# Weighted sums of v by plain f32 matmuls, two heads side by side in TensorE's columns, with separate denominators, in a linear-attention and two-layer feed-forward kernel

## The chip, the cores and the metric

The kernel runs on one core of a Trainium2 chip, as one program. The metric is device microseconds from the first to the last instruction. Three runs of the kernel before took 1057.39, 1061.38 and 1066.32 us; the median is 1061.38 us.

## The reference

Attention with exponential features instead of a softmax, then a gated feed-forward layer, then a second one with a leaky ReLU. Batch 4, 8 heads, 576 positions, head width 64, 128 projected features; all in float32.

```python
def phi(x):
    proj = np.einsum('bhsd,df->bhsf', x, w_phi)
    proj = proj - np.max(np.abs(proj), axis=-1, keepdims=True)
    return np.concatenate([np.exp(proj), np.exp(-proj)], axis=-1)
q_p, k_p = (phi(q), phi(k))
kv = np.einsum('bhsf,bhsd->bhfd', k_p, v)
z = np.sum(k_p, axis=2)
num = np.einsum('bhsf,bhfd->bhsd', q_p, kv)
den = np.einsum('bhsf,bhf->bhs', q_p, z)[..., None] + 1e-06
attn = num / den                                  # -> x: 2304 tokens x 512
gate = 1.0 / (1.0 + np.exp(-(x @ w_gate)))
x = gate * (x @ w_val) @ w_out                    # d_ff 1536
h = x @ w_in2
out = np.maximum(0.01 * h, h) @ w_out2            # d_ff 2048
```

## The kernel before

The program has two parts. The first, up to about 290 us, is attention, with most of the first chunk of the gated layer filled in between (pieces `M`, `up1` L205 and `down1` L235). The second part is the rest of both feed-forward layers; nothing of it is edited.

Attention works on 16 pairs of heads, 4 for each batch entry. The two heads of a pair lie together in most tiles. For each pair: k and q are loaded and transposed on TensorE (`transposed`, L324); multiplied with w_phi, which stands as a block diagonal for the two heads (`proj`, L337), with the row maximum and its subtraction on VectorE; k's features are exponentials on ScalarE (`features`, L352). `kv_main` (L389) sums k's features times v, and times a column of ones, over the positions: for each sign `s` of the exponent and each head one block of 128 features by 65 columns, 64 of v and one that holds the sum z. q's projections are transposed back and exponentiated (`q_f`, L410), so that features lie in partitions and the 576 positions in columns.

Then `num` (L433) multiplies: stationary is the block of `kv` (128 features; 65 columns used and 63 of zeros, so that the array's 128 columns are all taken), moving are 288 positions of q's features. The product has the weighted sums of v in 64 partitions and the denominator in a 65th. It is made for each head, each half `n` of the positions, and accumulated over the two signs: 8 products for a pair. For the second head the ones stand ahead of v, so that its sums land in partitions 64 to 127.

Precision comes in two forms. In a plain form, operands are float32. In the split form each operand is a rounded part (type float32r) and a remainder; `mm3` (L51) adds three matmuls (high x low weights and so on) and `split` (L47) makes the parts, the high one by a copy on ScalarE and the remainder by a subtraction on VectorE. `PLAIN_N` (L254) names the 8 of 16 pairs whose products in `num` are plain; the other 8 are split, for which `q_f` makes the exponentials twice on ScalarE (`qh` rounded, `qa` in full) and the remainder `ql` on VectorE (L430), and `kv_main` splits the block (`kvzr`).

`norm1` to `norm3` follow: the denominators are reshaped by a small DMA from one partition to 64 (tile `d`), 1e-6 is added and the reciprocal taken on VectorE, the result goes through DRAM and comes back broadcast over partitions (`rb`), GpSimd multiplies, and `norm3` splits the result into `xh` and `xl`, the feed-forward input.

The order of the pieces is a table: `ORDERS` holds lists of piece names (`tk` transposes k, `pk0` projects, `nn0` to `nn3` are the four steps of `num`, `nm1` to `nm3` the norm steps, `M` a unit of the gated layer, `d` a step of weight decoding, `ld` the next loads), `SLOTS` says which list each of 17 slots takes. In slot i the features of pair i, the sums of pair i-1 and `norm3` of pair i-2 are issued. The framework's scheduler reorders within each engine by its own estimate, so the engines' lists differ from the table. PSUM tiles of attention: a ring of three buffers `at` (transposes, projections), and `kv0`, `kv1` with one each, which the kv sums and the products of `num` share.

Of the kernel before, what the change touches and what calls it, by code (L numbers as in the profile page):

```python
# [19 lines left out]
def linear_attention_moe(ctx, tc, q, k, v, w_phi, w_gate, w_val, w_out, w_in2, w_out2, out):  # L20
# [233 lines left out]
    PLAIN_P, PLAIN_N = {0, 2}, {0, 1, 2, 3, 4, 5, 12, 14}  # L254
# [19 lines left out]

    kvzs = {}
    for nm, dts in (("f", (F32,)), ("r", (F32R, F32R))):
        kvzs[nm] = []
        for i in range(1):
            z = [wk.tile([128, 2, 256], dt, name=f"kvz{nm}{i}{j}") for j, dt in enumerate(dts)]
            for t in z:  # L280
                if nm == "f":
                    nc.gpsimd.memset(t[:, :, 65:128], 0.0)
                else:
                    nc.gpsimd.tensor_copy(t[:, :, 65:128], kvzs["f"][i][0][:, :, 65:128])
            kvzs[nm].append(z)
# [103 lines left out]
    def kv_main(p, s):  # L389

        ps = ps_a.tile([128, 2, 65], F32, tag=f"kv{s}", name="kv")
        vf = nat["v", p.b, p.c]
        for j in range(J):
            for h in range(2):
                nc.tensor.matmul(ps[:, h], p.kf[j // 2][:, j % 2, h, s, :], vf[:, j, 64 * h:64 * h + 65], start=(h, j) == (0, 0), stop=False)  # L395
        nc.tensor.matmul(ps.rearrange("p h w -> p (h w)"), rem["k"][:, 0, p.c % 2, s, :], vf[:, J], start=False, stop=True)
        zs = kvzs["f" if KD * p.b + p.c in PLAIN_N else "r"]
        p.kvz = zs[(KD * p.b + p.c) % len(zs)]
        part = [t[:, s].rearrange("p (h w) -> p h w", h=2)[:, :, 0:65] for t in p.kvz]
        if len(part) == 1:  # L400
            nc.scalar.copy(part[0], ps)
        else:
            split(ps, *part)
# [6 lines left out]
    def q_f(p, h):  # L410
# [8 lines left out]
        for sc in (1.0, -1.0):  # L419
            if KD * p.b + p.c in PLAIN_N:  # L420
                qf = wk.tile([128, S], F32, tag="qh", name="qf", bufs=4)
                exps(qf, sc)
                p.qf.append((qf,))
                continue
# [8 lines left out]
    def num(p, h):  # L433
        uh = wk.tile([128, S], F32, tag=f"u{h}", name=f"u{h}", bufs=2)
        for n in range(2):
            if n:
                yield
            cs = slice(288 * n, 288 * n + 288)
            ps2 = ps_a.tile([128, 288], F32, tag=f"kv{n}", name="ps_n")
            for s in range(2):  # L440
                i = 2 * h + s
                w = [z[:, s, 65 * h:65 * h + 128] for z in p.kvz]
                x = [f[:, cs] for f in p.qf[i]]
                if len(w) == 1:
                    nc.tensor.matmul(ps2, w[0], x[0], start=s == 0, stop=s == 1)  # L445
                else:
                    mm3(ps2, *w, *x, s == 0, s == 1)
            nc.scalar.copy(uh[:, cs], ps2)
        p.u.append(uh)

    def norm1(p):
        p.d = wk.tile([128, 9], F32, tag="d", name="d", bufs=2)
        for h in range(2):
            nc.sync.dma_start(out=p.d[64 * h:64 * h + 64], in_=p.u[h][64 - h:65 - h, :])

    def norm2(p):
        r = wk.tile([128, 9], F32, tag="r", name="r", bufs=2)
        nc.vector.tensor_scalar_add(p.d, p.d, 1e-6)
        nc.vector.reciprocal(r, p.d)
# [16 lines left out]
    def new_pair(b, c):  # L476
        p = Pair()
        p.b, p.c = b, c
        p.kf, p.tq, p.qf, p.u = [], [], [], []
# [25 lines left out]
    def step(gen, k=1):  # L505
# [15 lines left out]
    ]  # L521
    SLOTS = [0, 1, 2, 1, 5, 4, 3, 6, 3, 4, 3, 4, 3, 6, 5, 6, 3]
# [4 lines left out]
    for i in range(NP + 1):  # L527
# [9 lines left out]
        for piece in ORDERS[SLOTS[i]].split():  # L537
# [8 lines left out]
            elif piece[:2] == "nn":  # L546
                if o:
                    if piece[2:] in ("0", "2"):
                        ln = num(o, int(piece[2]) // 2)
# [499 lines left out]
```

## Time and profile before

| what | value |
|---|---|
| median of 3 runs | 1061.38 us |
| span of the profiled execution, its only time | 1055.6 us |
| busy share PE / PEld / DVE / ACT / POOL | 97% / 82% / 74% / 49% / 16% |
| mean granted TensorE clock | 0.997 |

The profile names engines PE (TensorE matmuls), PEld (its weight loads), DVE (VectorE), ACT (ScalarE), POOL (GpSimd), SP (SyncE, which issues DMAs). Busy time of matmuls includes the time in flight, and matmuls overlap, so how often one starts says more than how long one takes. A plain f32 matmul leaves two records, each with its own weight load; a transpose and an fp32r matmul leave one.

### The profile page before, as it was taken

To read this page: it belongs to the slowest core of one execution; us is meant where nothing else is said; L and a number is where in the kernel's file an instruction comes from. 1 tells how busy PE (TensorE), PEld (TensorE's weight loads), DVE (VectorE), ACT (ScalarE), POOL (GpSimd) and SP (SyncE) were. 2 spreads that over 40 slices of the span, in tenths; PEclk is the share of its full clock that TensorE was granted. 3 is DMA by queue.
4 is the path that set the end of the run, shared out by engine and by line. 5 is a ranking of instruction groups with operands and counts; after the bars stand their busy time and mean duration, and the time that the engine had idled before them with its cause. 6 is when DMAs were issued, how large, how long until landed. Compare 5 with 4: busy or idle time off the path is not lost.

```text
span 1055.6 us, 15004 instructions
## 1 busy us (share of the span) xinstructions
PE 1024.2 (97%) x5410; PEld 870.9 (82%) x5410; DVE 779.7 (74%) x1373; ACT 519.4 (49%) x1066; POOL 170.2 (16%) x217
## 2 busy tenths in 40 slices
PE   8999999999999989999999999899999999999998
PEld 7788989889788778888888878688888888888886
DVE  4964878766489748396684959998797887979555
ACT  4766676767456535454454434477343333433221
POOL 0112121212201123324144120001010010101000
PEclk9999999999999999999999999999999999999999
DMA  6543344332287978759499494536161542515143
GB/s 146 157 98 90 88 101 108 82 104 75 74 296 226 343 141 246 114 145 262 73 239 195 82 317 182 182 139 228 52 237 71 171 149 91 178 62 179 42 165 133
DMA packets 119481, 160.06 MB, mean 152 GB/s; under 512 B 68720, under 2 KB 71408, under 8 KB 119408
## 3 DMA queue, kind: packets, MB, share of 16 engines
q1 hardware_dynamic: 95216, 94.09, 28.5%
q0 software_dynamic: 24192, 65.02, 24.6%
q8 instruction: 43, 0.70, 0.3%
q14 instruction: 30, 0.25, 0.1%
HBM read 109.64 MB, written 49.36 MB: 151 GB/s over the span
## 4 chain that ended last, share of the span: by engine, by line
PE 81%; DVE 8%; DMA 5%; ACT 3%; issue 2%; SPq 1%; POOL 1%; POOLq 0%; DVEq 0%; ACTq 0%
PE ps_u L53 11%; PE ps_u L52 11%; PE ps_u L54 11%; PE ps_p L52 11%; PE ps_p L54 11%; PE ps_p L53 11%; PE kv L395 4%; PE ps_n L445 2%; DMA raw<-in_moe_w_gate_dram 1%; DMA acc<-xd 1%; PE ps_t L328 1%; DVE w L750 1%; DVE ql L430 1%; DVE acc L739 1%; DMA w<-td 1%
## 5 line engine op out<-in xcount | busy, mean ns | idle before, releaser
L831 DVE TENSOR_TENSOR q<-ps_u,q 128x512 f32<-128x512 f32 x160 | 109.6, 686 | 65.6 <-PE ps_u L54 59.4
L53 PE MATMUL ps_u<-xl,w 128*128 128x512 f32 (+1 forms) x432 | 151.6, 351 | 0.3 <-DVE xl L686 0.3
L52 PE MATMUL ps_u<-xh,w 128*128 128x512 f32 (+1 forms) x432 | 151.4, 351 | 0.1
L54 PE MATMUL ps_u<-xh,w 128*128 128x512 f32 (+1 forms) x432 | 150.9, 350 | 0.0
L901 DVE TENSOR_TENSOR acc<-acc,ps_p 128x512 f32<-128x512 f32 x126 | 86.1, 684 | 39.6 <-PE ps_p L54 39.0
L52 PE MATMUL ps_p<-w,gh 128*128 128x512 f32 x288 | 112.2, 390 | 0.0
L53 PE MATMUL ps_p<-w,gh 128*128 128x512 f32 x288 | 112.0, 389 | 0.0
L54 PE MATMUL ps_p<-w,gl 128*128 128x512 f32 x288 | 111.7, 389 | 0.0
L791 POOL DMA_DIRECT2D w<-td x88 | 48.7, 560 | 380.6 <-PE ps_u L54 365.2
L679 POOL DMA_DIRECT2D accd<-w x80 | 70.8, 892 | 229.2 <-ACT w L678 148.3
L52 PE MATMUL ps_u<-w 128*128 128x512 f32 x256 | 100.2, 391 | 1.6 <-DVE q L831 1.6
L53 PE MATMUL ps_u<-w 128*128 128x512 f32 x256 | 99.9, 390 | 0.7 <-DMA w<-td 0.7
L54 PE MATMUL ps_u<-w 128*128 128x512 f32 x256 | 99.7, 389 | 0.0
L52 PEld LDWEIGHTS ps_u<-xh,w 128*128 128x128 f32 x432 | 81.9, 190 | 11.9 <-DVE q L831 0.5
L53 PEld LDWEIGHTS ps_u<-xl,w 128*128 128x128 f32 x432 | 82.0, 190 | 11.4 <-DVE xl L686 0.5
L54 PEld LDWEIGHTS ps_u<-xh,w 128*128 128x128 f32 x432 | 81.9, 190 | 10.9
L52 PE MATMUL ps_p<-gh,w 128*128 128x512 f32 (+1 forms) x216 | 79.3, 373 | 10.3 <-ACT gh L48 4.8
L467 POOL TENSOR_TENSOR rb<-u,rb 64x576 f32<-64x576 f32 x32 | 49.2, 1537 | 233.8 <-DMA rb<-rd 136.3
L717 ACT ACTIVATE q<-q 128x512 f32<-128x512 f32 x48 | 30.2, 632 | 111.9 <-DVE q L831 111.6
L53 PE MATMUL ps_p<-gl,w 128*128 128x512 f32 (+1 forms) x216 | 80.1, 372 | 0.4 <-DVE gl L49 0.4
L54 PE MATMUL ps_p<-gh,w 128*128 128x512 f32 (+1 forms) x216 | 79.7, 370 | 0.0
L49 DVE TENSOR_TENSOR gl<-q,gh 128x512 fp32r<-128x512 f32 (+1 forms) x102 | 61.8, 613 | 20.6 <-ACT gh L48 20.2
(151 smaller groups left out, 2306.0 us busy)
## 6 DMA issues: line engine op xcount, KB each, us to landing
w<-td POOLq DMA_DIRECT2D x88, 512.0 KB, 6.5
td<-w SPq DMA_DIRECT2D x32, 512.0 KB, 5.2
accd<-w POOLq DMA_DIRECT2D x64, 256.0 KB, 6.1
raw<-in_moe_w_out_dram SPq DMA_DIRECT2D x28, 512.0 KB, 4.8
raw<-in_moe_w_in_dram SPq DMA_DIRECT2D x16, 512.0 KB, 4.1
raw<-in_moe_w_gate_dram SPq DMA_DIRECT2D x12, 512.0 KB, 5.9
raw<-in_moe_w_val_dram SPq DMA_DIRECT2D x12, 512.0 KB, 5.1
rb<-rd SPq DMA_DIRECT2D x32, 144.0 KB, 3.2
```

The source lines that it names most:

```text
L49: nc.vector.tensor_tensor(out=lo, in0=src, in1=hi.bitcast(F32), op=ALU.subtract)
L52: nc.tensor.matmul(ps, lh, rh, start=first, stop=False, **kw)
L53: nc.tensor.matmul(ps, lh, rl, start=False, stop=False, **kw)
L54: nc.tensor.matmul(ps, ll, rh, start=False, stop=last, **kw)
L395: nc.tensor.matmul(ps[:, h], p.kf[j // 2][:, j % 2, h, s, :], vf[:, j, 64 * h:64 * h + 65], start=(h, j) == (0, 0), stop=False)
L445: nc.tensor.matmul(ps2, w[0], x[0], start=s == 0, stop=s == 1)
L467: nc.gpsimd.tensor_tensor(out=p.rb[sl], in0=p.u[h][sl], in1=p.rb[sl], op=ALU.mult)
L679: nc.gpsimd.dma_start(out=accd[b][:, e], in_=st, accum_op=ALU.add)
L717: nc.scalar.activation(out=th, in_=t, func=ACTF.Lrelu)
L791: nc.gpsimd.dma_start(out=ts[n][k][0].bitcast(F32), in_=td[l, pair, n][:, k])
L831: nc.vector.tensor_tensor(out=o, in0=x, in1=y, op=ALU.add)
L901: nc.vector.tensor_tensor(out=a, in0=a, in1=po, op=ALU.add)
```

## The change

All 16 pairs become plain in `num`: `PLAIN_N`, the zero-padded tiles `kvzs`, the second exponentials and the remainders are gone. A matmul of `num` now has 64 stationary columns, the sums alone; the first head writes partitions 0 to 63 of a PSUM tile and the second 64 to 127, so they take different columns of the array, and the list alternates between the heads. The denominators get matmuls of their own: z of one head and sign, repeated in 32 columns, gives 32 equal partitions; head and sign choose which quarter of the columns. Nothing is accumulated over the signs there: both are copied to `dd`, fetched into two tiles `d0` and `d1`, and added on VectorE. The multiplication on GpSimd is one for both heads. The four steps of `num` are now two of sums and two of denominators.

```diff
@@ kv_main @@
-        zs = kvzs["f" if KD * p.b + p.c in PLAIN_N else "r"]
-        p.kvz = zs[(KD * p.b + p.c) % len(zs)]
-        part = [t[:, s].rearrange("p (h w) -> p h w", h=2)[:, :, 0:65] for t in p.kvz]
-        if len(part) == 1:
-            nc.scalar.copy(part[0], ps)
-        else:
-            split(ps, *part)
+        if s == 0:
+            p.kvz = wk.tile([128, 2, 2, 65], F32, tag="kvz", name="kvz", bufs=2)
+        nc.scalar.copy(p.kvz[:, s], ps)
@@ q_f @@
-            a = wk.tile([128, S], F32, tag="qa", name="qa", bufs=2)
-            qh = wk.tile([128, S], F32R, tag="qh", name="qh", bufs=4)
-            ql = wk.tile([128, S], F32R, tag="ql", name="ql", bufs=4)
-            exps(qh, sc)
-            exps(a, sc)
-            nc.vector.tensor_tensor(out=ql, in0=a, in1=qh.bitcast(F32), op=ALU.subtract)
-            p.qf.append((qh, ql))
+            qf = wk.tile([128, S], F32, tag="qf", name="qf", bufs=6)
+            exps(qf, sc)
+            p.qf.append(qf)
@@ num @@
-            ps2 = ps_a.tile([128, 288], F32, tag=f"kv{n}", name="ps_n")
-            for s in range(2):
-                i = 2 * h + s
-                w = [z[:, s, 65 * h:65 * h + 128] for z in p.kvz]
-                x = [f[:, cs] for f in p.qf[i]]
-                if len(w) == 1:
-                    nc.tensor.matmul(ps2, w[0], x[0], start=s == 0, stop=s == 1)
-                else:
-                    mm3(ps2, *w, *x, s == 0, s == 1)
-            nc.scalar.copy(uh[:, cs], ps2)
+    HS = [(h, s) for s in range(2) for h in range(2)]
...
+        for n, cs in enumerate(halves):
+            ps2 = ps_a.tile([128, 288], F32, tag=f"kv{n}", name="ps_n")
+            for h, s in HS:
+                nc.tensor.matmul(ps2[64 * h:64 * h + 64], p.kvz[:, s, h, h:h + 64], p.qf[2 * h + s][:, cs], start=s == 0, stop=s == 1)
+            nc.scalar.copy(p.u[:, cs], ps2)
+            yield
+        p.dd = wk.tile([128, S], F32, tag="dd", name="dd", bufs=2)
+        for n, cs in enumerate(halves):
+            ps3 = ps_a.tile([128, 288], F32, tag="at", name="ps_d", bufs=3)
+            for h, s in HS:
+                i = 2 * h + s
+                z = p.kvz[:, s, h, 64 * (1 - h):64 * (1 - h) + 1].to_broadcast([128, 32])
+                nc.tensor.matmul(ps3[32 * i:32 * i + 32], z, p.qf[i][:, cs], start=True, stop=True)
+            nc.scalar.copy(p.dd[:, cs], ps3)
+            yield
@@ norm1, norm2 @@
-        p.d = wk.tile([128, 9], F32, tag="d", name="d", bufs=2)
-        for h in range(2):
-            nc.sync.dma_start(out=p.d[64 * h:64 * h + 64], in_=p.u[h][64 - h:65 - h, :])
+        p.d = [wk.tile([128, 9], F32, tag=f"d{s}", name=f"d{s}", bufs=2) for s in range(2)]
+        for s in range(2):
+            for h in range(2):
+                i = 32 * (2 * h + s)
+                nc.sync.dma_start(out=p.d[s][64 * h:64 * h + 64], in_=p.dd[i:i + 1, :])
...
-        nc.vector.tensor_scalar_add(p.d, p.d, 1e-6)
+        nc.vector.scalar_tensor_tensor(out=p.d[0], in0=p.d[0], scalar=1e-6, in1=p.d[1], op0=ALU.add, op1=ALU.add)
...
-        for h in range(2):
-            sl = slice(64 * h, 64 * h + 64)
-            nc.gpsimd.tensor_tensor(out=p.rb[sl], in0=p.u[h][sl], in1=p.rb[sl], op=ALU.mult)
+        nc.gpsimd.tensor_tensor(out=p.rb, in0=p.u, in1=p.rb, op=ALU.mult)
@@ tables @@
-    SLOTS = [0, 1, 2, 1, 5, 4, 3, 6, 3, 4, 3, 4, 3, 6, 5, 6, 3]
+    SLOTS = [0, 1, 1, 2, 3, 4, 5, 6, 5, 4, 3, 4, 3, 7, 3, 3, 8]
```

`ORDERS` is rewritten, with nine lists in place of seven. Slots 1 and 2 have no `d` any more, slot 3 has all of them, and what is left is issued ahead of slot 4; from slot 4 on `M` stands 69 times in place of 64.

TensorE's list around the products of pair 8 (the first of batch entry 2), before. `ps_n` is the PSUM tile of a product, `qh`, `ql` and `kvzr` its split operands, `ps_p` a projection of the next pair, `pv` a tile of the gated layer:

```order
L53 MATMUL ps_n_1988<-ql_1888,kvzr00_140 128x288
L52 MATMUL ps_p_2004<-wbh_113,xhi_1968 128x256
L53 MATMUL ps_p_2004<-wbl_114,xhi_1968 128x256
L54 MATMUL pv_2351<-xh10_82,w_399 128x512
L54 MATMUL ps_n_1988<-qh_1887,kvzr01_141 128x288
L52 MATMUL ps_n_1996<-qh_1879,kvzr00_140 128x288
L53 MATMUL ps_n_1996<-ql_1880,kvzr00_140 128x288
L54 MATMUL ps_n_1996<-qh_1879,kvzr01_141 128x288
L52 MATMUL ps_n_1996<-qh_1887,kvzr00_140 128x288
L53 MATMUL ps_n_1996<-ql_1888,kvzr00_140 128x288
```

And of the changed kernel, the same pair. `ps_d` is the tile of the denominators; the four `qf` of a tile are head 0 and 1 with the first sign, then with the second:

```order
L416 MATMUL ps_n_1973<-qf_1884,kvz_1915 64x288
L416 MATMUL ps_n_1973<-qf_1899,kvz_1915 64x288
L416 MATMUL ps_n_1973<-qf_1887,kvz_1915 64x288
L416 MATMUL ps_n_1973<-qf_1902,kvz_1915 64x288
L416 MATMUL ps_n_1979<-qf_1884,kvz_1915 64x288
L416 MATMUL ps_n_1979<-qf_1899,kvz_1915 64x288
L416 MATMUL ps_n_1979<-qf_1887,kvz_1915 64x288
L416 MATMUL ps_n_1979<-qf_1902,kvz_1915 64x288
L425 MATMUL ps_d_1986<-qf_1884,kvz_1915 32x288
L425 MATMUL ps_d_1986<-qf_1899,kvz_1915 32x288
L425 MATMUL ps_d_1986<-qf_1887,kvz_1915 32x288
L425 MATMUL ps_d_1986<-qf_1902,kvz_1915 32x288
```

In place of three matmuls for each of eight products there are eight matmuls of 64 columns and eight of 32 (four more stand a few rows further down). Here the eight are unbroken; over the whole list the 128 matmuls of 64 columns stand in 38 runs and those of 32 columns in 30, with 124 changes of width.

VectorE's list where pair 8 gets its features, before. `m` is a row maximum, `t` and `tq` the projections less that, `kvzr01` the remainder of the kv block, `xlo` a remainder of the next pair's transposed k or q:

```order
L349 TENSOR_TENSOR tq_1862<-ps_p_1853,m_1860 128x512
L49 TENSOR_TENSOR kvzr01_141<-kv_1925,kvzr00_140 128x2x65
L430 TENSOR_TENSOR ql_1880<-qa_1878,qh_1879 128x576
L430 TENSOR_TENSOR ql_1888<-qa_1886,qh_1887 128x576
L430 TENSOR_TENSOR ql_1911<-qa_1909,qh_1910 128x576
L430 TENSOR_TENSOR ql_1919<-qa_1917,qh_1918 128x576
L49 TENSOR_TENSOR kvzr01_141<-kv_1951,kvzr00_140 128x2x65
L49 TENSOR_TENSOR xlo_1969<-ps_t_1963,xhi_1968 128x512
```

And of the changed kernel:

```order
L337 TENSOR_TENSOR tq_1854<-ps_p_1845,m_1852 128x512
L439 RECIPROCAL r_1817<-d0_1796 128x9
L335 TENSOR_REDUCE m_1863<-ps_p_1856 128x4
L337 TENSOR_TENSOR t_1865<-ps_p_1856,m_1863 128x512
L49 TENSOR_TENSOR xlo_1960<-ps_t_1954,xhi_1959 128x512
```

The six subtractions between the last projection and the next pair's `xlo` are gone; the reciprocal and a projection of k stand there.

## Rows read from the trace of the kernel before

**Rows 1.** The page, part 1: busy us (share of the span) x instructions

```profile
PE 1024.2 (97%) x5410; PEld 870.9 (82%) x5410; DVE 779.7 (74%) x1373; ACT 519.4 (49%) x1066; POOL 170.2 (16%) x217
```

**Rows 2.** Busy time by stretch: us, busy us (x instructions) by engine, clock, DMA

```profile
20.00:60.00 40.00, 35.53 (x226) 29.30 (x226) 34.76 (x67) 28.26 (x72) 2.95 (x2) 1.00 0.55 137
60.00:285.00 225.00, 218.35 (x1530) 196.44 (x1530) 152.78 (x282) 145.86 (x399) 45.32 (x30) 1.00 0.35 91
285.00:1055.60 770.60, 753.54 (x3580) 630.62 (x3579) 585.13 (x1012) 338.79 (x584) 119.91 (x169) 1.00 0.59 170
```

**Rows 3.** The chain in order of time, end of attention: start us, us

```profile
290.17 0.60 ACT st L226
...
290.78 0.32 SPq L229
...
291.15 6.49 DMA raw<-in_moe_w_gate_dram
...
297.67 0.43 DVE e L102
```

**Rows 4.** Waits of PE, 20 to 285 us: total us, times, longest us

```profile
PE ps_n L53 <- DVE ql L430: 2.1, 3, 1.2
...
PE ps_n L445 <- ACT qf L416: 1.3, 2, 0.7
PE ps_p L52 <- DVE xl L49: 1.2, 1, 1.2
...
PE ps_n L54 <- DVE kvzr L49: 0.9, 1, 0.9
```

**Rows 5.** Groups: busy us, mean ns of one | idle us before, releasers

```profile
L395 PE MATMUL kv<-vf,ka 128*128 128x65 f32 x512 | 63.2, 270 | 0.0
...
L467 POOL TENSOR_TENSOR rb<-u,rb 64x576 f32<-64x576 f32 x32 | 49.2, 1537 | 233.8 <-DMA rb<-rd 136.3 <-ACT qa L417 38.9 <-DVE xlo L49 18.0
...
L445 PE MATMUL ps_n<-qf,kvzf 128*128 128x288 f32 x128 | 37.8, 412 | 1.4 <-ACT qf L416 1.3
...
L430 DVE TENSOR_TENSOR ql<-qa,qh 128x576 fp32r<-128x576 f32 x32 | 34.6, 1096 | 18.8 <-ACT qa L416 12.5 <-ACT qa L417 6.2
...
L448 ACT COPY u<-ps_n 128x288 f32<-128x288 f32 x64 | 27.0, 441 | 16.5 <-PE ps_n L54 9.6 <-PE ps_n L445 6.6
...
L416 ACT ACTIVATE qa<-ps_q 128x512 f32<-128x512 f32 x32 | 21.0, 657 | 0.5 <-DVE ql L430 0.5
...
L52 PE MATMUL ps_n<-qh,kvzr 128*128 128x288 f32 x64 | 20.0, 315 | 0.0
...
L53 PE MATMUL ps_n<-ql,kvzr 128*128 128x288 f32 x64 | 19.6, 309 | 2.1 <-DVE ql L430 2.1
...
L54 PE MATMUL ps_n<-qh,kvzr 128*128 128x288 f32 x64 | 19.2, 302 | 0.9 <-DVE kvzr L49 0.9
...
L417 ACT ACTIVATE qa<-ps_r 128x64 f32<-128x64 f32 x32 | 9.3, 290 | 0.0
...
L49 DVE TENSOR_TENSOR kvzr<-kv,kvzr 128x130 fp32r<-128x130 f32 x16 | 4.6, 290 | 5.9 <-ACT kvzr L48 5.9
```

**Rows 6.** Tile ps_n: duration ns min/median/max, first and last start us

```profile
L445 PE MATMUL ps_n<-qf,kvzf x128: 403/406/510, 22.9 to 261.0; 128*128 128x288 f32 x128
```

**Rows 7.** Timeline of PE: start us, us; a run's last is in it

```profile
42.84 1.62 PE L445 MATMUL ps_n<-qf,kvzf 128*128 128x288 f32 x6
44.30 0.60 PE L328 MATMUL ps_t<-ident,q 128*128 128x128 f32 x4
...
48.83 2.34 PE L395 MATMUL kv<-vf,ka 128*128 128x65 f32 x20
```

**Rows 8.** Timeline of PE, fp32r products of one pair, every one a row

```profile
125.32 0.29 PE L53 MATMUL ps_n<-ql,kvzr 128*128 128x288 f32 x1
...
126.91 0.29 PE L53 MATMUL ps_n<-ql,kvzr 128*128 128x288 f32 x1
```

**Rows 9.** DMA issues: KB each, median us to landing

```profile
d<-u SPq DMA_DIRECT2D x32, 2.2 KB, 2.0
```

More of the change, by code (lines that the diff above doesn't have):

```diff
@@ L250, in linear_attention_moe @@
     ps_a = att.enter_context(tc.tile_pool(name="ps_a", bufs=1, space=PS))
-    PLAIN_P, PLAIN_N = {0, 2}, {0, 1, 2, 3, 4, 5, 12, 14}
+    PLAIN_P = {0, 2}
     wbd = wk.tile([128, 2 * NF], F32, name="wbd")
@@ L273, in linear_attention_moe @@
         vfs.append(vf)
[L275 to L282, printed above, removed]
-                else:
-                    nc.gpsimd.tensor_copy(t[:, :, 65:128], kvzs["f"][i][0][:, :, 65:128])
-            kvzs[nm].append(z)
     nat = {}
@@ L430, in q_f @@
-            nc.vector.tensor_tensor(out=ql, in0=a, in1=qh.bitcast(F32), op=ALU.subtract)
-            p.qf.append((qh, ql))
[L433 to L438, printed above, removed]
-            ps2 = ps_a.tile([128, 288], F32, tag=f"kv{n}", name="ps_n")
-            for s in range(2):
-                i = 2 * h + s
-                w = [z[:, s, 65 * h:65 * h + 128] for z in p.kvz]
-                x = [f[:, cs] for f in p.qf[i]]
-                if len(w) == 1:
-                    nc.tensor.matmul(ps2, w[0], x[0], start=s == 0, stop=s == 1)
-                else:
-                    mm3(ps2, *w, *x, s == 0, s == 1)
-            nc.scalar.copy(uh[:, cs], ps2)
-        p.u.append(uh)
@@ L451, in norm1, with num @@
-    def norm1(p):
-        p.d = wk.tile([128, 9], F32, tag="d", name="d", bufs=2)
-        for h in range(2):
-            nc.sync.dma_start(out=p.d[64 * h:64 * h + 64], in_=p.u[h][64 - h:65 - h, :])
+            qf = wk.tile([128, S], F32, tag="qf", name="qf", bufs=6)
+            exps(qf, sc)
+            p.qf.append(qf)
+    HS = [(h, s) for s in range(2) for h in range(2)]
+    def num(p):
+        p.u = wk.tile([128, S], F32, tag="u", name="u", bufs=2)
+        halves = [slice(288 * n, 288 * n + 288) for n in range(2)]
+        for n, cs in enumerate(halves):
+            ps2 = ps_a.tile([128, 288], F32, tag=f"kv{n}", name="ps_n")
+            for h, s in HS:
[6 more added lines that the diff above has]
+            for h, s in HS:
+                i = 2 * h + s
+                z = p.kvz[:, s, h, 64 * (1 - h):64 * (1 - h) + 1].to_broadcast([128, 32])
+                nc.tensor.matmul(ps3[32 * i:32 * i + 32], z, p.qf[i][:, cs], start=True, stop=True)
+            nc.scalar.copy(p.dd[:, cs], ps3)
+            yield
@@ L456, in norm2 @@
+    def norm1(p):
+        p.d = [wk.tile([128, 9], F32, tag=f"d{s}", name=f"d{s}", bufs=2) for s in range(2)]
[3 more added lines that the diff above has]
+                nc.sync.dma_start(out=p.d[s][64 * h:64 * h + 64], in_=p.dd[i:i + 1, :])
     def norm2(p):
         r = wk.tile([128, 9], F32, tag="r", name="r", bufs=2)
-        nc.vector.tensor_scalar_add(p.d, p.d, 1e-6)
-        nc.vector.reciprocal(r, p.d)
+        nc.vector.scalar_tensor_tensor(out=p.d[0], in0=p.d[0], scalar=1e-6, in1=p.d[1], op0=ALU.add, op1=ALU.add)
+        nc.vector.reciprocal(r, p.d[0])
@@ L478, in new_pair @@
         p.b, p.c = b, c
-        p.kf, p.tq, p.qf, p.u = [], [], [], []
+        p.kf, p.tq, p.qf = [], [], []
         return p
@@ L547, in linear_attention_moe @@
                 if o:
-                    if piece[2:] in ("0", "2"):
-                        ln = num(o, int(piece[2]) // 2)
+                    if piece[2:] == "0":
+                        ln = num(o)
                     next(ln, None)
```

5 lines of the change are left out of this document (removed), and 16 rows, old and new, of the table ORDERS.

## Prediction

> **What bounds the kernel now.** I read the engines' totals first, then busy time by stretch, then the end of attention in the chain, then who kept TensorE waiting, and last the rows of the instructions that the change touches. TensorE is busy 97% of the span, VectorE 74%, ScalarE 49% [rows 1]. By stretch the change can reach only what runs up to about 290 us: the last copy of that part starts at 290.17 us, and after it the chain goes through a store, a weight fetch of 6.49 us and the first decode step of the next part [rows 3]. Nothing of the feed-forward part can start its decoding earlier, so whatever attention gains or loses shifts the rest by the same amount; I count it at full price.
>
> Inside attention TensorE is the bound, with some holes. Between 20 and 60 us it is busy 35.53 of 40 us and VectorE 34.76; between 60 and 285 us it is busy 218.35 of 225 us, VectorE 152.78, ScalarE 145.86 [rows 2]. Its idle time from 20 to 285 us is thus 4.47 + 6.65 = 11.1 us. Of that, 2.1 us waited for the remainders ql, 0.9 us for the low half kvzr, 1.3 us for the exponentials qf [rows 4].
>
> **Its own time.** The durations are those of an execution with a span of 1055.6 us, the only time of it that is shown, the last end in [rows 2]; the median of the runs is 1061.38 us, 5.8 us above. I work out a difference from the rows and put it on the median.
>
> **Term 1: TensorE's work for the weighted sums.** A plain f32 matmul is two passes on this engine (64 instructions, 128 records) [rows 5]. Six such passes take 1.62 us from first start to last end, and one takes 0.406 us in the median, so they start every (1.62 - 0.406) / 5 = 0.243 us [rows 6, 7]. A single-pass matmul on fp32r of the same 288 columns starts every (126.91 - 125.32) / 12 = 0.1325 us [rows 8]. Before: 128 plain passes at 0.243 are 31.1 us, and 3 x 64 = 192 fp32r passes at 0.1325 are 25.4 us [rows 5]; together 56.5 us. After: each of 16 pairs has 8 matmuls of 64 columns for the sums and 8 of 32 columns for the denominators, all plain, so 256 matmuls or 512 passes. One after another they are 512 x 0.243 = 124.4 us.
>
> How much of this runs side by side no row of before shows, since every matmul there uses all 128 columns. The order of the changed program gives the neighbours: 128 matmuls of 64 columns stand in 38 unbroken runs, and counted off in twos within their runs they need 76 slots; the 128 denominators stand in fours and need 32. If all neighbours in different columns overlap wholly, the work is (76 + 32) x 2 x 0.243 = 52.5 us, that is 4.0 us less than before. If TensorE starts passes strictly in the order of its list, the other head's first pass can begin only beside the second pass of the head ahead of it: one pass is hidden for each of the 183 neighbours in other columns, which leaves 124.4 - 183 x 0.243 = 79.9 us, 23.4 us more than before. If nothing overlaps it is 67.9 us more. I take -4.0 us. The nearest row for that is the run of 20 passes of 65 columns, which start every (2.34 - 0.27) / 19 = 0.109 us though one takes 0.270 us [rows 5, 7]: two or three are in the array at once, and the next always stands ready when the one ahead leaves room. A second pass that waits for its own columns need not hold up a pass for free columns. That is a choice, not a reading, and the ends -4.0 and +23.4 stay in the range.
>
> **Term 2: changes between whole and split columns.** The order has 124 places where a matmul of one column width follows one of another. The trace has no such place. A pass stays 0.406 - 0.243 = 0.163 us in the array after its successor of equal shape has started; if each change waits for that, it is 124 x 0.163 = 20.2 us, and from below it is 0 (no reason makes it a gain). I take 0.05 us each, 6.2 us, nearer to the lower end, because weights are loaded within 0.109 us before a pass anyway [rows 7], which covers part of the wait. The weight loads of the narrow matmuls I put at nothing: a full load keeps pace with 0.109 us, under a pass of 0.243 us. If a narrow load can't run ahead of the pass before it, that is up to 183 x 0.109 = 20 us.
>
> **Term 3: what the other engines give back.** VectorE loses 32 remainders of 1.096 us and 16 of 0.290 us: 39.7 us [rows 5], all in the eight pairs that were not plain. ScalarE loses 32 second exponentials of 0.657 and 0.290 us, 30.3 us; its copies out of PSUM stay 64 of 288 columns, half of them now denominators [rows 5]. GpSimd multiplies once with 128 partitions in place of twice with 64, 1.537 us less for each pair [rows 5], on the path from the denominator to the split of x. All this is off TensorE's path but for the waits. The waits on ql and kvzr (3.0 us) go for certain; all 11.1 us is the ceiling. I take 9 us, near the ceiling, since after 60 us VectorE falls from 68% of the time to about half. What is late next are TensorE's own tiles: the denominators take two more tiles of the three-buffer ring that transposes and projections use, and the copy that frees one takes 0.441 us [rows 5]. With two other buffers I put that at nothing; if every one of the 32 showed, it would be 14 us.
>
> The first six pairs were plain already, so nothing is freed up to 60 us; there the same work of the split stands in another order, and the decoding steps are asked for in the fourth slot alone, though the order still has the first of them after the first pair's projections. I put it at nothing; the idle 4.47 us of that stretch bounds it from below, the same again from above.
>
> SyncE issues four small loads of denominators in place of two for each pair. One lands in 2.0 us [rows 9]; two more issues lie ahead of the reciprocal's store on SyncE's queue, and the loads of the next pair are behind them. GpSimd's 1.5 us pays for it, so I count both at nothing. The add of 1e-6 becomes an add of two tiles of the same nine columns, with nothing in it.
>
> **Sum.** -4.0 + 6.2 - 9 = -6.8 us; 1061.4 - 6.8 = 1054.6 us, as the likeliest.
>
> **Rivals.**
>
> *Strict order.* TensorE holds a free column group back while an earlier pass waits. For it: in the 2.1 us of idle time on ql no later matmul went ahead of the one that waited [rows 4]. Against it: a matmul there waited for data, not for columns. It decides from the point where term 1 comes to +2.8 us in place of -4.0 us, the amount that the other two terms can pay for: a quarter of the way from full overlap to this one. Here +23.4 + 6.2 - 10 = +19.6 us, 1081 us: slower. The Trainium skill, "TensorE: Matmul & The Clock Gate", Part 3 (Packing small matmuls), states that matmuls start and end in the program's order, and gives 2.38 times for three column tiles; no run here shows either. By that rule with two passes for each matmul it is this rival and not my forecast.
>
> *Full drain at each change of width.* -4.0 + 20.2 - 8 = +8 us, 1070 us. For it: the 0.163 us are real. Against: where transposes follow the six plain passes, the first starts at 44.30 us, 0.245 us after the sixth pass (42.84 + 5 x 0.243 = 44.06 us), so a change of kind alone costs nothing [rows 7]. The Trainium skill, "TensorEngine Tiling (Array Packing)", Key Properties, says that a change of the tiling mode drains the engine; no row of before has one. By that rule it is this rival.
>
> *No price for the changes and all waits gone.* -4.0 + 0 - 11.1 = -15.1 us, 1046 us. For it: the change of kind that costs nothing [rows 7]. Against: some waits, as 1.2 us on xl, have nothing to do with what is removed [rows 4].
>
> *The columns don't run side by side.* +67.9 + 6.2 - 11.1 = +63 us, 1124 us. For it: no overlap is seen before. Against: an array that has two or three passes in flight.
>
> **How the numbers follow.** A measurement of this kernel can tell about 1% (10.6 us) from no change. Forecast 0.34: half of it faster by over 1%, half within. No price 0.22, nearly all faster. Strict order 0.27: 0.23 slower, 0.04 within. Full drain 0.10: 0.07 within, 0.03 slower. No overlap 0.07, slower. That makes 0.38 faster, 0.28 within 1%, 0.34 slower. The forecast's own range is 1046 to 1063 us. The whole range goes from 1042 us (no price, and some of the first stretch's idle gone) to 1090 us (strict order with part of the weight loads showing), and leaves out the last rival and the far ends.
>
> **What would show it.** In the profile after: passes of the second head that start within some 0.01 to 0.06 us of the first head's (full overlap), 0.243 us later (strict order) or 0.486 us later (none); four denominators in about 0.5 us, 1.2 us or 1.9 us. A gap ahead of the first 64-column pass after a transpose, over 0.1 us, would show the drain. No remainders ql, and VectorE near half busy from 60 us on. The last copy of the first part should come near 283 us instead of 290.17 us, and the rest be shifted by as much. I am wrong in the main if that copy comes after 290 us, or if the part behind it changes its length by more than 5 us.

## The result, and the profile after

The changed kernel takes **1070.51 us** (median of 10 runs, 1063.18 to 1072.68) against 1061.05 us of the kernel before (10 runs of its own): ratio 1.0080, 95% interval 1.0057 to 1.0103. It is slower by 0.8%, a real difference, though within the 1% that the prediction counted as no change. The forecast was 1054.6 us, with a range of its own of 1046 to 1063 us; the measured time lies above that, and within the whole range, which went to 1090 us.

The profiled execution spans 1069.6 us, 14.0 more than the one shown before. Page, part 1, of the changed kernel, which answers to [rows 1]:

```profile
PE 1039.7 (97%) x5602; PEld 851.3 (80%) x5602; DVE 743.9 (70%) x1325; ACT 503.4 (47%) x1002; POOL 143.4 (13%) x198
```

VectorE and GpSimd give back 36 and 27 us, near the forecast 39.7 and 16 x 1.537 = 24.6 us; ScalarE gives back 16 us, about half of its 30.3. TensorE has 15.5 us more. By stretch, to read against [rows 2] (the column behind POOL is the granted clock):

```profile
20.00:60.00 40.00, 34.90 (x233) 24.49 (x231) 27.04 (x52) 22.64 (x58) 1.41 (x1) 0.96 0.48 126
60.00:285.00 225.00, 221.87 (x1648) 171.73 (x1647) 122.22 (x242) 131.12 (x335) 19.85 (x14) 0.98 0.36 93
```

TensorE's idle time from 20 to 285 us fell from 11.1 to 5.10 + 3.13 = 8.2 us, 2.9 us less. New is the clock: it was 1.00 in both stretches and is 0.96 and 0.98. The execution shown before had a mean clock of 0.997, which no run of that kernel on record exceeds; this one has 0.990, the mean of the change's ten runs. This is one reason why the two lie 14.0 us apart, and the medians 9.5. The chain shows the end of attention:

```profile
300.78 0.60 ACT st L226
```

That copy started at 290.17 us [rows 3]; attention ends 10.6 us later, and the part behind it grew from 765.4 to 768.8 us. What TensorE waited for from 20 to 285 us (total us, times, longest), against [rows 4]:

```profile
PE ps_p L54 <- DVE xlo L49: 4.5, 1, 4.5
PE pg L52 <- ACT xh L48: 2.1, 1, 2.1
...
PE ps_n L416 <- ACT qf L400: 0.2, 1, 0.2
```

The waits for ql and kvzr are gone as forecast, and two new ones stand in their place. Around them TensorE runs at the lower of its two clock levels (1.2 GHz), which it did in neither stretch of attention in the execution shown before. Two windows of the changed kernel, same columns as [rows 2]:

```profile
27.82:31.23 3.41, 3.06 (x18) 2.41 (x18) 2.71 (x5) 0.46 (x2) 0.00 (x0) 0.50 0.81 218
85.85:92.68 6.83, 6.83 (x29) 6.34 (x29) 2.85 (x8) 1.81 (x4) 0.00 (x0) 0.50 0.19 39
```

The timeline of TensorE has the ends of the two waits (idle time ahead in brackets):

```profile
28.17 0.58 PE L54 MATMUL ps_p<-wbh,xlo 128*128 128x256 f32 x1 [4.47 <-DVE xlo L49]
...
84.25 0.50 PE L52 MATMUL pg<-xh,w 128*128 128x512 f32 x1 [2.05 <-ACT xh L48]
```

The first half-clock stretch begins 0.35 us ahead of the first wait's end, the second 1.6 us behind the second. The two cost (3.41 + 6.83) / 2 = 5.1 us. The whole execution loses 1069.6 x 0.010 = 10.7 us to the clock, so over half of it lies behind attention, in the part that was not edited; the execution before lost 1055.6 x 0.003 = 3.2 us, all of it there. Now the narrow passes themselves, one pair in the timeline of TensorE (start us, us from first start to last end):

```profile
164.39 0.60 PE L316 MATMUL ps_t<-ident,q 128*128 128x128 f32 x4
164.92 2.16 PE L416 MATMUL ps_n<-qf,kvz 128*64 128x288 f32 x16
167.01 0.69 PE L425 MATMUL ps_d<-qf,kvz 128*32 128x288 f32 x8
167.63 0.39 PE L52 MATMUL ps_p<-wbh,xhi 128*128 128x256 f32 x1
```

Sixteen passes of 64 columns need 167.01 - 164.92 = 2.09 us. A pass starts every 0.243 us; eight times that would be 1.94, sixteen times 3.89, so the two heads do run side by side; in the record their passes start 6 to 7 ns apart. The four denominators (eight passes, four at once) need 0.62 us; twice 0.243 would be 0.49. Call the time of two passes, 0.486 us, a slot. Within these groups the overlap is complete, and each is 0.13 to 0.15 us longer than its slots. It is not complete everywhere. Here is a run of four 64-column matmuls as it should be, and another:

```profile
234.84 1.19 PE L416 MATMUL ps_n<-qf,kvz 128*64 128x288 f32 x8
235.96 0.69 PE L425 MATMUL ps_d<-qf,kvz 128*32 128x288 f32 x8
```

```profile
74.99 1.67 PE L416 MATMUL ps_n<-qf,kvz 128*64 128x288 f32 x8
76.59 0.69 PE L425 MATMUL ps_d<-qf,kvz 128*32 128x288 f32 x8
```

The first takes 235.96 - 234.84 = 1.12 us, two slots (0.97 us) and the 0.15. The second takes 1.60 us, three slots, as three matmuls of one head and one of the other would; the rows don't name the head. Five of the 38 runs are like that, so the sums take 81 slots and not the 76 of the prediction.

### The profile page after: what moved, and what is told of

Read it like the earlier page. It is cut to its first block, busy times and chain, and to the rows that moved or that the text cites. A ratio compares the mean times of both kernels' runs of the same rounds, so it can differ in the third digit from the quotient of the medians.

```text
span 1069.6 us, 15289 instructions
## 1 busy us (share of the span) xinstructions
PE 1039.7 (97%) x5602; PEld 851.3 (80%) x5602; DVE 743.9 (70%) x1325; ACT 503.4 (47%) x1002; POOL 143.4 (13%) x198
## 4 chain that ended last, share of the span: by engine, by line
PE 77%; DMA 7%; issue 6%; DVE 5%; POOL 3%; SPq 1%; ACT 1%; POOLq 0%; DVEq 0%; ACTq 0%
PE ps_u L53 10%; PE ps_p L52 10%; PE ps_u L54 10%; PE ps_u L52 10%; PE ps_p L54 10%; PE ps_p L53 10%; PE kv L383 5%; PE ps_n L416 3%; DMA rb<-rd 2%; POOL accd L659 2%; PE ps_d L425 1%; PE ps_t L316 1%; PE ps_q L397 1%; DMA rd<-r 1%; DMA raw<-in_moe_w_gate_dram 1%
## 5 line engine op out<-in xcount | busy, mean ns | idle before, releaser
L53 PEld LDWEIGHTS ps_u<-xl,w 128*128 128x128 f32 x432 | 82.7, 191 | 12.5 <-DVE xl L666 0.8
L54 PEld LDWEIGHTS ps_u<-xh,w 128*128 128x128 f32 x432 | 82.6, 191 | 10.8
L52 PE MATMUL ps_p<-gh,w 128*128 128x512 f32 (+1 forms) x216 | 79.0, 373 | 11.1 <-ACT gh L48 4.8
L103 ACT ACTIVATE e<-e,ebias 128x512 int32<-128x512 int32 x68 | 49.1, 725 | 45.9 <-DVE e L102 45.6
```

The lines of the kernel that those rows point to most:

```text
L52: nc.tensor.matmul(ps, lh, rh, start=first, stop=False, **kw)
L53: nc.tensor.matmul(ps, lh, rl, start=False, stop=False, **kw)
L54: nc.tensor.matmul(ps, ll, rh, start=False, stop=last, **kw)
L103: nc.scalar.activation(out=e, in_=e, func=ACTF.Relu, scale=8.0, bias=ebias)
```

## The experiments

Theory A says that the loss is the price of changes of column width (124 of them); theory B that it comes of the new order, through the new waits and the half clock around them. Each timed run lists its span and its mean granted clock. Their product, span times clock, takes out what running at half clock cost, as far as TensorE is the bound there; span less product is that cost. For the ten runs of the kernel before that stand beside the change no clock is on record. Over its 57 runs beside these experiments that kernel has a product of 1050.7 us and loses 7.3; the changed kernel (10 runs) has 1057.2 and loses 10.8. So **6.5 us of the loss are there at full clock, and 3.5 us are clock.** The last two columns are from the one traced execution of each run: the slots that its sums and denominators take on TensorE, read from the lengths of the runs of narrow matmuls (a whole matmul is one slot), and TensorE's idle time from 20 to 285 us, which was 11.1 us before.

| run | width changes | ratio to before (95%) | product, us | lost to the clock, us | slots | idle, us |
|---|---|---|---|---|---|---|
| the change | 124 | 1.0080 (1.0057 to 1.0103) | 1057.2 | 10.8 | 113 | 8.2 |
| e1_old_order | 131 | 1.0146 (1.0117 to 1.0175) | 1060.8 | 12.3 | 113 | 5.3 |
| e2_plain_whole | 0 | 1.0037 (1.0020 to 1.0055) | 1053.5 | 9.1 | 128 | 10.6 |
| e3_plain_whole_new_order | 0 | 1.0107 (1.0078 to 1.0136) | 1058.9 | 10.9 | 128 | 17.9 |
| e4_bunched | 63 | 1.0134 (1.0109 to 1.0160) | 1059.3 | 13.4 | 96 | 21.8 |
| e5_first_old | 114 | 1.0078 (1.0052 to 1.0103) | 1057.5 | 9.0 | 109 | 8.8 |
| e6_first_new | 141 | 1.0131 (1.0098 to 1.0165) | 1060.7 | 11.4 | 116 | 7.2 |
| e7_bunched_chain | 54 | 1.0078 (1.0047 to 1.0109) | 1051.3 | 15.7 | 96 | 18.4 |
| e8_bunched_first_old | 54 | 1.0062 (1.0036 to 1.0087) | 1051.5 | 12.5 | 96 | 15.4 |
| e9_bunched_old | 48 | 1.0099 (1.0067 to 1.0132) | 1052.7 | 15.0 | 96 | 15.0 |
| e10_tiny_narrow | 128 | 1.0230 (1.0204 to 1.0257) | 1071.9 | 10.1 | 128 and 64 short matmuls | 5.4 |
| e11_tiny_whole | 0 | 1.0158 (1.0134 to 1.0182) | 1063.3 | 11.0 | 128 and 64 short matmuls | 9.3 |

**Sums and order apart (e1, e2, e3).** The first run keeps the new sums and takes back the order:

```diff
-    SLOTS = [0, 1, 1, 2, 3, 4, 5, 6, 5, 4, 3, 4, 3, 7, 3, 3, 8]
+    SLOTS = [0, 1, 2, 1, 5, 4, 3, 6, 3, 4, 3, 4, 3, 6, 5, 6, 3]
...
```

> The changed kernel with the tables ORDERS and SLOTS of the kernel before: only the sums of v are new (64 and 32 columns, plain f32), nothing else is moved. Two theories. Theory A: the loss is the price of the changes of column width on TensorE (about 0.16 us each as the changed kernel's rows read: 124 of them, 20 us, against 4.0 saved by the passes side by side); the order is worth nothing. It has 131 changes here, 7 more, so A expects the time of the changed kernel and 1 us more: 1070 to 1073 us. Theory B: the loss is the new order: PE waited 4.5 us for xlo and 2.1 us for xh, and ran 10.2 us at half clock right behind these two waits (5.1 us lost); the change of width is paid by the relief of VectorE and ScalarE. B expects some 10 us less than the changed kernel: 1057 to 1062 us.

The second keeps the old order and one whole matmul per head, but plain f32 in all pairs; the third adds the new tables to it:

```diff
-    PLAIN_P, PLAIN_N = {0, 2}, {0, 1, 2, 3, 4, 5, 12, 14}
+    PLAIN_P, PLAIN_N = {0, 2}, set(range(16))
```

> The kernel before with all 16 pairs' sums in plain f32 (they were 8 of 16), still one whole-array matmul for a head with its 65th column, the old order: no change of column width at all, and VectorE and ScalarE relieved as in the change. TensorE's passes: 16 x 8 matmuls of 0.486 us = 62.2 us against 56.5 before, +5.7. Relief of the other engines by the prediction -3 to -11. Theory A: 1061 + 5.7 - 3 to 11 = 1056 to 1064 us, and the first experiment lies 8 to 14 us above it (21 us of width changes less 9.7 us of passes saved). Theory B: the same 1056 to 1064 us, but the first experiment lies below it, by up to 9.7 us.

> The same as the one before (all sums whole, plain f32), with the ORDERS and SLOTS of the changed kernel: the order alone. Theory A: within 2 us of the old order's (1056 to 1064 us). Theory B: 8 to 12 us above it (1066 to 1074 us), with PE waits for xlo and xh and the half-clock stretches behind them in the first 100 us.

Measured medians: 1076.43, 1064.47 and 1071.45 us. With the old order the packed sums cost 1060.8 - 1053.5 = 7.3 us more at full clock than whole ones, though their 15 slots less save 7.3 (9.7 by the 108 slots that were forecast): theory A's sign, at 14.6 us for 131 changes. With the new order they cost 1.7 us less (the change against e3), so 5.6 us for 124: 0.11 and 0.05 us a change. That is net of waiting: where TensorE has the narrow matmuls it idles less, 5.3 against 10.6 us in the old order and 8.2 against 17.9 in the new one. With this counted, the price is (14.6 + 5.3) / 131 = 0.15 and (5.6 + 9.7) / 124 = 0.12 us a change. Theory B falls in its simple form, since e1 is slower than the change and not faster; A's 1070 to 1073 us was too low by 3 us. But the order is not worth nothing either, as A had it: it saves 3.6 us of product with packed sums (e1 to the change) and costs 5.4 with whole ones (e2 to e3). In e3 B's waits are there:

```profile
PE ps_p L52 <- DVE t L349: 6.4, 4, 2.3
PE ps_p L54 <- DVE xlo L49: 5.8, 1, 5.8
```

The second run also prices the relief of the other engines alone. Its passes are 5.7 us more than before, and its product is 2.8 us more: VectorE's and ScalarE's relief is worth **2.9 us**, net of the waits that it brings itself (in its trace TensorE idles 10.6 us, 0.5 less than before).

**The price of a change by itself (m1).** One engine, fixed order, constant data; the reference's work is left out:

```diff
+    whole(48)
...
+    for _ in range(N):
+        whole()
+        pair()
+    for _ in range(N):
+        whole()
+        quad()
+    for _ in range(N):
+        pair()
+        quad()
...
+    for _ in range(N):
+        pair("0011")
...
```

> No attention at all: the reference's work is left out whole, and TensorE alone runs matmuls of the change's sizes on constant data in a fixed order, so that the price of a change of column width can be read by itself. Blocks of 8: whole plain f32 matmuls (128 columns, 288 moved), groups of four 64-column ones as the change lists them (h0 h1 h0 h1), of four 32-column ones, of four transposes; then whole and narrow by turns. Theory A (a change drains the array): whole 0.486 us each, a 64-column group 0.486, a 32-column group 0.486 (two passes, four at once); whole and 64-column group by turns 0.486 + 0.486 + 2 x 0.10 to 0.16 = 1.17 to 1.29 us a turn; with 32 columns the same; 64 and 32 by turns also 1.17 to 1.29; four transposes and a 64-column group 0.44 + 0.49 + 0.2 to 0.32; transposes and a whole matmul 0.92 without a price. Theory C (a change costs nothing by itself, and what the changed kernel shows comes of its waits and narrow weight loads): 0.97 us a turn. The groups listed h0 h0 h1 h1: 0.49 us if each half of the columns takes its own passes ahead of the other half's, 0.73 or more if passes start in the order of the list.

The expectation counted a 64-column group wrongly: four matmuls of two passes, two at once, are two slots, 0.97 us and not 0.486; its sums of a turn are to be raised by that. The timeline of TensorE, first the blocks of one kind (32 transposes, 8 groups of 64 columns, 8 of 32, 16 fp32r matmuls), then turns of whole and 64, whole and 32, 64 and 32, transposes and 64, fp32r and 64, the block h0 h0 h1 h1, and transposes with whole matmuls:

```profile
29.47 3.66 PE L64 MATMUL pt<-w 128*128 128x128 f32 x32
33.05 7.98 PE L55 MATMUL pb<-x,w 128*64 128x288 f32 x64
40.96 4.09 PE L60 MATMUL pc<-x,w 128*32 128x288 f32 x64
44.98 2.37 PE L49 MATMUL pr<-xr,wr 128*128 128x288 f32 x16
47.19 0.65 PE L45 MATMUL pa<-x,w 128*128 128x288 f32 x2
47.77 1.19 PE L55 MATMUL pb<-x,w 128*64 128x288 f32 x8
48.89 0.75 PE L45 MATMUL pa<-x,w 128*128 128x288 f32 x2
49.57 1.19 PE L55 MATMUL pb<-x,w 128*64 128x288 f32 x8
...
62.19 0.69 PE L60 MATMUL pc<-x,w 128*32 128x288 f32 x8
62.81 0.75 PE L45 MATMUL pa<-x,w 128*128 128x288 f32 x2
63.50 0.69 PE L60 MATMUL pc<-x,w 128*32 128x288 f32 x8
...
71.95 1.19 PE L55 MATMUL pb<-x,w 128*64 128x288 f32 x8
73.07 0.69 PE L60 MATMUL pc<-x,w 128*32 128x288 f32 x8
73.69 1.19 PE L55 MATMUL pb<-x,w 128*64 128x288 f32 x8
...
85.90 0.66 PE L64 MATMUL pt<-w 128*128 128x128 f32 x4
86.48 1.19 PE L55 MATMUL pb<-x,w 128*64 128x288 f32 x8
87.60 0.66 PE L64 MATMUL pt<-w 128*128 128x128 f32 x4
...
99.55 0.53 PE L49 MATMUL pr<-xr,wr 128*128 128x288 f32 x2
100.01 1.19 PE L55 MATMUL pb<-x,w 128*64 128x288 f32 x8
101.13 0.53 PE L49 MATMUL pr<-xr,wr 128*128 128x288 f32 x2
...
111.09 9.00 PE L55 MATMUL pb<-x,w 128*64 128x288 f32 x72
120.02 1.24 PE L45 MATMUL pa<-x,w 128*128 128x288 f32 x4
...
139.36 0.60 PE L64 MATMUL pt<-w 128*128 128x128 f32 x4
139.80 0.65 PE L45 MATMUL pa<-x,w 128*128 128x288 f32 x2
140.28 0.38 PE L64 MATMUL pt<-w 128*128 128x128 f32 x2
```

Read starts, not lengths. Alone a 64-column group takes (40.96 - 33.05) / 8 = 0.99 us, a 32-column group 0.50 and four transposes 0.45. Each of these blocks ends in a change of its own, an eighth of which is in such a mean; without it they are the slots, 0.97 and 0.49, and 139.80 - 139.36 = 0.44 us. A whole matmul is two passes of 0.243 [rows 6, 7], 0.49 us, and two fp32r matmuls are 0.27 [rows 8]. By turns, against the slots:

- whole and 64: 49.57 - 47.77 = 1.80 us, 0.34 over its parts, **0.17 us a change**
- whole and 32: 1.31, 0.34 over, 0.17 a change
- 64 and 32: 1.74, 0.28 over, 0.14 a change
- transposes and 64: 1.70, 0.29 over, 0.15 a change
- fp32r and 64: 1.58, 0.34 over, 0.17 a change
- transposes and whole matmuls, a change of kind and not of width: 140.28 - 139.36 = 0.92 against 0.92, nothing (the view ends inside the last row)

Theory C is out. The clock was 1.00 in all these stretches, so the changes don't lower it here. The groups listed h0 h0 h1 h1 take (120.02 - 111.09 - 1.12) / 8 = 0.98 us (1.12 is the group of the turn before), as long as h0 h1 h0 h1. Started in the order of the list, two of a group's eight passes could be hidden, and it would take 6 x 0.243 = 1.46. A half of the columns thus takes its next pass while an earlier-listed one waits for the other half. This rests on the engine's list standing as the kernel asks for it, since the rows don't name the half.

**Where the order counts (e5, e6).** The tables are mixed: e5 has the old order in steps 0 to 3 and the new one behind, e6 the other way round.

```diff
-    SLOTS = [0, 1, 1, 2, 3, 4, 5, 6, 5, 4, 3, 4, 3, 7, 3, 3, 8]
+    SLOTS = [0, 1, 2, 1, 3, 4, 5, 6, 5, 4, 3, 4, 3, 7, 3, 3, 8]
...
```

> The changed kernel with the order of the kernel before in the first four steps (the first 90 us, with the decoding of weights in steps 1 and 2), the new order in the other thirteen: 114 changes of width. Theory A alone (the price of 114 changes, 10 fewer): 1 to 2 us less than the changed kernel, 1068 to 1070 us. Theory B in its narrower form (the new order loses only in the first stretch, by the waits for xlo and xh, 6.6 us, and the 10.2 us at half clock behind them, 5.1 us, and wins behind it): 8 to 11 us less, 1060 to 1063 us.

> The other half: the new order in the first four steps, the order of before behind them: 141 changes of width. Theory A alone: 17 more changes than the changed kernel, 2 to 3 us more, 1072 to 1074 us. Theory B: the lossy stretch of the new order with the old order's rest (the first experiment, all old, took 1076): 1080 us or more, with the wait for xlo and half-clock stretches before 100 us.

Medians 1067.75 and 1074.40 us, both misses for B: with the wait for xlo gone e5 has the change's product (1057.5 against 1057.2) and recovers at most 1.8 us of clock; with it e6 is no slower than e1. The first 90 us decide nothing at full clock. The new order's 3 us lie in the later thirteen steps. That it hurts whole sums shows in e3's idle time, 7.3 us more than e2's. Why it helps packed ones, with 2.9 us more idle time than e1, was not tried further.

**Fewer changes (e4, e7, e8, e9).** A pair's sixteen narrow matmuls are issued as one piece, with heads and signs in reverse order, in e4 with high priority, in the others chained and, in most steps, behind pk0; e8 and e9 copy dd ahead of u and have the old order in the first four steps or in all.

```diff
+        ps2 = [ps_a.tile([128, 288], F32, tag=f"kv{n}", name="ps_n") for n in range(2)]
...
-                nc.tensor.matmul(ps2[64 * h:64 * h + 64], p.kvz[:, s, h, h:h + 64], p.qf[2 * h + s][:, cs], start=s == 0, stop=s == 1)
-            nc.scalar.copy(p.u[:, cs], ps2)
-            yield
+                mm = nc.tensor.matmul(ps2[n][64 * h:64 * h + 64], p.kvz[:, s, h, h:h + 64], p.qf[2 * h + s][:, cs], start=s == HS[0][1], stop=s == HS[3][1])
+                tc.keep_in_program_order(mm)
...
```

> The changed kernel, but the eight 64-column and eight 32-column passes of a pair are issued as one piece at nn0 with high priority, so that less stands between them: 63 changes of width in place of 124, the order table as in the change. Theory A: 61 x 0.16 = 9.8 us less than the changed kernel, 1059 to 1063 us; the matmul groups of 64 and 32 columns look the same per instruction in the bunch, fewer gaps of 0.1 us stand at the ends. Theory B: as the changed kernel, 1068 to 1073 us, as the waits for xlo and xh stay.

> Bunched again, without the high priority that made PE wait for qf and dd in the bunched run: a pair's sixteen narrow passes stand in one piece on TensorE, behind the piece pk0 in most steps, the copies behind them; 54 changes of width. Theory A: 70 changes less than the changed kernel at 0.10 to 0.16 us = 7 to 11 us less, 1059 to 1064 us, if PE's idle time stays at the changed kernel's 9 us. If the passes in one piece have to wait for the last of the four exponentials of q, and the copy of dd comes late, PE's idle time grows by as much as the changes give back (as in the bunched run: 23.1 us in place of 9.0), and it takes 1068 to 1073 us.

> The narrow passes of a pair in one piece (54 changes of width, as in the chained run), with the old order in the first four steps, so that the 6.8 us wait for xlo of the chained run goes, and the copies of dd ahead of those of u, so that the next step's projections get their PSUM slot sooner (1.9 us there). Theory A (the price of the changes, 0.13 to 0.17 us each by the run of widths alone): the fifth run has this order with 114 changes; 60 fewer are 8 to 10 us less at full clock. The time times the granted clock, which takes the half-clock loss out, was 1057.5 us there and 1051.3 in the chained run; it should be 1045 to 1050 here, and the time, with 8 to 14 us lost at half clock, 1056 to 1063 us. If the changes were not the loss, it stays at 1066 to 1069 us.

> The same with the old order in all seventeen steps, 48 changes of width against 131 in the first experiment. Theory A: 83 x 0.13 to 0.17 = 11 to 14 us less at full clock than the first experiment's 1060.8 us, 1047 to 1050, and 1057 to 1064 us in time. Theory B' (the new order of the later steps is worth 6 us whatever the bunching, as the first and the fifth run differ): 6 us above the run before this one. If the new order helps only by where it puts single narrow passes, the two are within 3 us.

Medians 1074.73, 1067.80, 1065.40 and 1069.06 us. The first is a miss for A: TensorE's busy time fell from 1039.7 to 1031.3 us, and waits took its place (4.2 us on xlo, 3.6 us on xh, 4.2 us on dd). The other three bear A's sign out at full clock. From e5 to e8, at one order but for the place of nn0 and of two copies, 60 changes less bring 5.9 us; from e1 to e9, 83 less bring 8.1 us. Two things are mixed with the changes here. A matmul that stands alone takes a whole slot for half of the columns, so the bunch also needs fewer slots, 96 for 109 and 113: 6.3 and 8.3 us. And it brings waits: TensorE idles 6.6 and 9.7 us more. With both counted, (5.9 - 6.3 + 6.6) / 60 = 0.10 and (8.1 - 8.3 + 9.7) / 83 = 0.11: **about 0.10 us a change**, by difference. e8 misses its product of 1045 to 1050 us by 1.5 and e9 its 1047 to 1050 by 2.7, since A had not counted the waits; their times miss by 2 and 5 us, with the half clock on top. e7's time, 1067.80 us, is at the edge of its second case, the one with waits (1068 to 1073 us), and not in A's 1059 to 1064. The wait list of TensorE in e8, 0 to 300 us, shows them:

```profile
PE ps_t L316 <- ACT qf L400: 6.6, 8, 2.8
PE ps_p L52 <- ACT dd L427: 3.3, 6, 1.0
```

The transposes and projections of the next pair find no free PSUM tile until the exponentials and copies of this one are done. The order's gain is down to 1.2 us (e9 less e8), so most of it was where single narrow passes stood. At full clock e7 and e8 are level with the kernel before, and they lose 5 to 8 us more than it to half clock. No version here beats the kernel before.

**Changes put into whole sums (e10, e11).** One short matmul ahead of each of the 64 groups of e2, narrow in e10 and whole in e11, at the same places; in both the sums keep the program's order, which in e2 they need not:

```diff
-                    nc.tensor.matmul(ps2, w[0], x[0], start=s == 0, stop=s == 1)
+                    if s == 0:
+                        nc.tensor.matmul(ps2[0:64, 0:8], w[0][:, 0:64], x[0][:, 0:8], start=True, stop=True)
+                    tc.keep_in_program_order(nc.tensor.matmul(ps2, w[0], x[0], start=s == 0, stop=s == 1))
```

> All sums whole in plain f32 with the old order (the second experiment), and ahead of each of the 64 groups of sums one more matmul that moves 8 columns of q into 64 columns of the array, overwritten by the group itself: 128 changes of width where there were none, nothing else moved. Theory A: the 64 matmuls themselves (some 0.1 us each, two short passes) 4 to 8 us, and 128 x 0.126 to 0.17 us = 16 to 22 us of changes, less what lies in waits that TensorE has anyway: 1064 + 18 to 30 = 1082 to 1094 us; against the control that follows, +12 to +22 us. If a change of width costs nothing in the kernel, it takes as long as the control.

> The control: the same 64 short matmuls at the same places of TensorE's order, in all 128 columns of the array, so without a change of width. Every theory: 1064 + 4 to 8 (the matmuls themselves) + up to 4 (64 more weight loads that can show) = 1068 to 1076 us.

Medians 1083.85 and 1075.98 us, products 8.6 us apart: 0.067 us a change. The times are 7.9 us apart, and 12 to 22 were expected. The control is dear itself, 9.8 us over e2 or 0.15 us for each short matmul. The tile ps_n of e10 and then of e11 (ns min/median/max):

```profile
L446 PE MATMUL ps_n<-qf,kvzf x128: 202/223/273, 21.7 to 292.1; 128*64 128x8 f32 x128
```

```profile
L446 PE MATMUL ps_n<-qf,kvzf x128: 170/256/381, 22.9 to 284.6; 128*128 128x8 f32 x128
```

The whole one is up to 381 ns in flight with 8 columns moved. That it waits for weights, which a pass too short can't hide, and that this takes the place of part of the price, is argued and not shown. Against e2, without the control, the 64 narrow ones cost 18.4 us, 0.14 us a change with their own passes in it.

## Why the prediction was wrong

**Term 1 held in its mechanism.** The choice of full overlap was right against the ends +23.4 and +67.9, though 113 slots in place of 108 leave -1.6 us of its -4.0: starts 6 to 7 ns apart, and the mark of 0.5 us for four denominators met but for the change of width (0.62). *Strict order* and *no overlap* are out. The reason given for the choice, that a pass for free columns need not wait, is what the block h0 h0 h1 h1 shows. There the Trainium skill, "TensorE: Matmul & The Clock Gate", Part 3 (Packing small matmuls), says that matmuls start strictly in program order; this measurement (0.98 us, where that order would give 1.46) differs from it, and decides.

**Term 2 was the step that failed.** It took 0.05 us a change, 6.2 us, "because weights are loaded within 0.109 us before a pass anyway". The array alone pays 0.14 to 0.17 us, about the 0.163 us that were the upper end, one pass's time left in flight. In the kernel it comes to 0.10 to 0.15 us by the differences of runs with slots and waits counted (e10 against its dear control: 0.067); 0.10 is 12.4 us for 124. The argument against the drain (transposes that follow plain passes without a gap) showed a change of kind, and m1 shows that kind costs nothing while width does: the row was read for something that it doesn't hold. The Trainium skill, "TensorEngine Tiling (Array Packing)", Key Properties, that a change of tiling mode drains the engine, agrees in that such a change costs time, 0.14 to 0.17 us here.

**Term 3 was sized by the ceiling.** -9 us was taken; the idle time between 20 and 285 us fell by 2.9 us, and e2 prices the relief alone at 2.9 us: about the 3.0 us of ql and kvzr that it called certain. Lower busy shares elsewhere did not shorten TensorE's other waits, and new ones came.

**Nothing for the order and nothing for the clock.** The order was worth -3.6 us, and in the later steps, where the prediction had not weighed it; the first stretch, for which it kept +-4.47 us, gave nothing. The clock was not in the sum at all: 3.5 us.

Put together with the measured sizes: -1.6 + 12.4 - 2.9 = +7.9 us at full clock, where 6.5 were measured, and 3.5 us of clock: +11.4 for +9.5 us. That is as close as these differences go. The order stands outside this sum. By the same working e1, with 113 slots and 131 changes, has +8.6, and +10.1 were measured. How much of the 3.5 us the new waits brought is not shown, since over half of what the traced execution lost lies behind attention.

**The rival that gave 1070 us**, *full drain at each change of width*, had the right mechanism and landed on the measured time. Its terms did not: its 20.2 us of price are what the array alone pays, but 12.4 show in the kernel, its overlap of -4.0 us was -1.6, its relief of 8 us was 2.9, and its clock loss was nothing. That the errors cancelled was luck. Its chance of 0.10 was too small. The mark set for the drain, a gap of over 0.1 us ahead of the first 64-column pass, was too coarse: that pass starts 164.92 - (164.39 + 3 x 0.109) = 0.20 us behind the last transpose, 0.09 more than the 0.109 of [rows 7]; the rest of the price shows behind it, in the group's length and on the way back. The copy at the end of attention comes after 290 us, and this alone said that the forecast was wrong in the main.

## What to carry to other kernels

When small matmuls are packed side by side, count the places where the width changes, not only the passes saved, and price each near the time that a pass stays in flight after its successor could have started (0.163 us here, against 0.14 to 0.17 measured). Count the slots in the list as it stands, for a narrow matmul without a neighbour fills one by itself. Bunching the narrow passes brings both down, but a bunch waits for its last operand and holds more PSUM tiles, and what TensorE then idles can come back again as half clock. Relief of engines off the path is worth the waits on them that the list names, not the busy time that they lose.

## What had not been expected of the hardware

The halves of the columns take their passes side by side: two 64-column passes start 6 to 7 ns apart, and listing h0 h0 h1 h1 costs nothing. A change of width costs 0.14 to 0.17 us; a change from matmul to transpose or back, nothing. The clock moved the times by as much as the edits did: the kernels here lose 7.3 to 15.7 us to it, mean by mean. In the changed kernel the half clock came with idle time (4.47 and 2.05 us), and m1, with no idle time, stayed at 1.00. But the same wait for tq, 1.55 us in the kernel before and 1.44 in e1, was followed by half clock in e1 alone:

```profile
55.17 1.38 PE L397 MATMUL ps_q<-ident,tq 128*128 128x128 f32 x8 [1.44 <-DVE tq L337]
```

```profile
56.94:60.35 3.41, 3.41 (x12) 1.55 (x13) 0.66 (x1) 2.22 (x7) 0.00 (x0) 0.50 0.04 6
```

What decides which wait is followed by it stays open.
